# Weights of the first expert tile split by other engines, and two turns of rows moved by two steps

## Chip, core and metric

The kernel runs on one core of a Trainium2 chip. The metric is the device time of one execution in microseconds (us). Engines are named TensorE (PE, with its weight loads as PEld), VectorE (DVE), ScalarE (ACT), GpSimd (POOL) and SyncE (SP, which only issues transfers here).

## What is computed

Attention with rotary embedding over 4 batches, 8 heads, 576 tokens and 64 dimensions a head, and behind it a mixture of 8 experts with one expert for each token. A token keeps the expert of its predecessor unless its local gate is under 0.5.

```python
scores = scale * np.matmul(q_rot, k_rot.transpose(0, 1, 3, 2))
attn = softmax(scores)                    # over the keys
x = np.matmul(attn, v)                    # joined over the heads: 4 x 576 x 512
...
e = fresh_e if s == 0 or local_gate[b, s] < 0.5 else prev_e
h = np.maximum(x[b, s] @ w1[e], 0.0)      # 512 -> 1024
out[b, s] = p[e] * (h @ w2[e])            # 1024 -> 512
```

## The kernel before

The first part (to about 300 us) is the attention, 16 pairs of heads in 9 steps each. Its results go as rows to memory, and for the first three batches the tokens are sorted by expert. The second part works on tiles of 128 sorted tokens of one expert. The first six (`KE`) hold tokens of the first three batches alone, so that they can start while the routing of the fourth batch is still being worked out.

The work of a tile t:

- `gather(t)` (L893) fetches its 128 rows by an indirect DMA from POOL's queue.
- `turn_x(t)` transposes the rows on TensorE (L904, tile `tx`) and splits the result (L300 and L304): the high part of `xs` is a cast by ScalarE, the low part a subtraction by VectorE, with one input in PSUM and one in SBUF.
- `split_w(t, c)` makes high and low parts of pieces 2c and 2c+1 of the expert's eight weight pieces (128 x 1024 each; 0 to 3 are W1, 4 to 7 W2). The high part is a cast by ScalarE (L863) or an operation of POOL (L865), the low part a subtraction by VectorE or POOL (both L866), with both inputs in SBUF. `SPLITS[t]` says which: the first list names the pieces whose high part is ScalarE's, the second those whose low part is POOL's; all other high parts are POOL's, all other low parts VectorE's. For tile 0 the pieces 0 and 1 are split by POOL earlier (L835, L836). If a tile has the same expert as the one before, the split is skipped; only piece 0 and 1 of tile 1 are split whatever its expert.
- `first_product(t)` (L915, tile `h`) multiplies by W1, in four steps of six matmuls, one step for each piece: two with the high parts of rows and weights, two with the weights' low part, two with the rows' low part. A Relu (L919, tile `hr`) on ScalarE follows.
- `turn_h(t)` (L928, tiles `th`) transposes the inner rows, eight transposes, and splits them into `hs` as above.
- `second_product(t)` (L937, tile `o`) multiplies by W2, in four steps of six, and a scatter (L943) writes the rows.

The tiles overlap. For the first six, `TILE_EARLY[t]` is the order in which the steps are written down: f a step of the first product of tile t (the fifth is the Relu), s a step of the second product of tile t-1, x `turn_x(t + 1)`, A and B `split_w(t + 1, 0 and 1)`, C and D `split_w(t, 2 and 3)`, h `turn_h(t)`, g the gathers of tiles 4 and 5 at tile 0.

For these tiles TensorE and VectorE take their instructions in exactly this order; ScalarE, POOL and SP are ordered by a scheduler. In between stands the routing of the fourth batch (L467 to L611, small VectorE operations with a few TensorE and ScalarE ones). It has no place of its own in the string: each split by `split_to`, and each piece whose low part is VectorE's, first takes up to three of its operations (`pull(PULL)`). So a step that moves takes operations of the routing with it. The ones that matter here are, in this order, L467 and L485 (reductions), L488 (128 x 40, both inputs in SBUF), L491 (ScalarE), L496 and L498 (both inputs in SBUF), L501 (a reduction) and L504.

Of the kernel before, what the change touches and what calls it, by code (L numbers as in the profile page):

```python
# [44 lines left out]
QK_LAST = 121  # L45
SPREAD_LAST = 127

TILE_EARLY = ("ffAffsfxBssgCsshD", "ffAffxfsBsCsgsshD", "fffAffxBssChsgssD", "ffAfffxBsssshsCDg", "ffAfffBsssxsshCgD", "fffxAffsBssgssChD")
TILE = "ffAgffxBsfsshsCDs"
TILE_LAST = "ffxAfffssBsChsDss"  # L50
PULL = 3
# [5 lines left out]
DX = DM + 1  # L57
GATES_AT = {13: 4, 14: 7, 15: 4}

SPLITS = (((1, 2, 3, 4, 5, 7), (0, 6)), ((0, 3, 5, 6, 7), (1, 5, 6)), ((3, 4, 5, 6), (1, 5, 6)), ((1, 3, 4, 7), (1, 3, 4)), ((0, 2, 4, 5, 6), (5, 6)), ((3,), (0, 7)), ((2, 5, 6, 7), (4,)))  # L60
ACT_ROWS = False
ZTHR = -1.5 * 2.0 ** -23

# [72 lines left out]
def tile_attention_moe(ctx, tc, qk, v, tabs, turn, consts, tri, wg, wts, out):  # L136
# [162 lines left out]
    def split_to(hi, lo, src, wait=False):  # L299
        act.copy(hi, src)  # L300
        pull(PULL)

        def rest():
            dve.tensor_tensor(lo, src, hi.bitcast(F32), op=ALU.subtract)  # L304

        return rest if wait else rest()
# [100 lines left out]
    def finish():  # L407
        side["slots"] = 0
        for _ in side["parts"]:
            pass  # L410
# [397 lines left out]
    def expert_of(t):  # L808
        regs[t] = (
            sp.value_load(meta[0:1, t:t + 1], min_val=0, max_val=NE - 1),  # L810
            sp.value_load(meta[0:1, 32 + t:33 + t], min_val=0, max_val=1),
        )
# [29 lines left out]
    def needs_of(t):  # L842

        need_t[t] = nc.values_load_multi_w_load_instructions(
            meta[0:1, 32 + t:33 + t], engines=(act.engine, dve.engine, pool.engine), min_val=0, max_val=1)[1][0]

    def split_w(t, c):

        if c not in w_own:
            w = pt_p.tile([P, 2, 4, S], F32R, tag="pt", name=f"w_{c}")  # L850
            w_own[c] = w.rearrange("p a k s -> p (a k s)")[:, 0:4096].rearrange("p (c l n) -> p c l n", c=2, l=2)
            held = False
        else:
            held = t in need_t
        w = w_own[c]
        on_act, on_pool = SPLITS[min(t, KE)]

        def parts():
            for d in range(2):
                k = 2 * c + d  # L860
                src, hi, lo = staged(k), w[:, d, 0], w[:, d, 1]
                if k in on_act:
                    act.copy(hi, src)  # L863
                else:
                    pool.tensor_scalar(hi, src, 1.0, 1.0, op0=ALU.mult, op1=ALU.mult)  # L865
                (pool if k in on_pool else dve).tensor_tensor(lo, src, hi.bitcast(F32), op=ALU.subtract)  # L866

        for k in (2 * c, 2 * c + 1):
            if k not in on_pool:
                pull(PULL)  # L870
        if held:
            with tc.If(need_t[t] > 0):  # L872
                parts()
        else:
            parts()
        for d in range(2):
            k = 2 * c + d
            w_t[t, k] = w[:, d, 0], w[:, d, 1]
            w_done.add((t, k))
            load_w(t + 1, k)  # L880

    def gather(t):
        if t < 4:
            if t == 0:
                x_t[-1] = over.tile([P, 4, S], F32, tag="xq", name="x_0")
            x = x_t[-1][:, t]
        elif t < KE:
            x = over.tile([P, 1024], F32, tag=f"qst{t - 4}", name=f"x_{t}")
        else:
            x = xt_p.tile([P, S], F32, tag="xt", name=f"x_{t}")  # L890

        top = NT - S if t < KE else NT
        pool.indirect_dma_start(  # L893
            out=x[:, 0:DX], out_offset=None, in_=rows_d[0:top + 1],
            in_offset=bass.IndirectOffsetOnAxis(ap=gidx[:, t:t + 1], axis=0),
            bounds_check=top, oob_is_err=False)
        x_t[t] = x

    def turn_x(t, wait=False):
        xs = v2_p.tile([P, 10, 2, D], F32R, tag="v2", name=f"xs_{t}")  # L900
        xs = xs.rearrange("p j c d -> p (j c d)")[:, 0:1024].rearrange("p (l k n) -> p l k n", l=2, k=4)
        ps = ps_t.tile([P, 4, P], F32, tag="t", name=f"tx_{t}")
        for k in range(4):
            pe.transpose(ps[:, k], x_t[t][:, k * P:(k + 1) * P], ident)  # L904
        xs_t[t] = xs
        lo = split_to(xs[:, 0], xs[:, 1], ps, wait)
        return lo

    def first_product(t):
        ps = ps_s.tile([P, 2, 512], F32, tag="s", name=f"h_{t}")  # L910
        for k in range(4):
            w = w_t.pop((t, k))
            for n, (x, y) in enumerate(PASSES):
                for c in range(2):
                    pe.matmul(ps[:, c], xs_t[t][:, x, k], w[y][:, c * 512:(c + 1) * 512],  # L915
                              start=(k == 0 and n == 0), stop=(k == 3 and n == 2))
            yield k
        h = ej_p.tile([P, 2, S], F32, tag="ej", name=f"hr_{t}").rearrange("p a s -> p (a s)")[:, 0:1024]
        act.activation(h, ps.rearrange("p c n -> p (c n)"), AF.Relu)  # L919
        h_t[t] = h  # L920

    def turn_h(t):
        hs = m_p.tile([P, 2, 2, S], F32R, tag="m", name=f"hs_{t}")
        hs = hs.rearrange("p a c s -> p (a c s)")[:, 0:2048].rearrange("p (l k n) -> p l k n", l=2, k=8)
        for c in range(2):
            ps = ps_t.tile([P, 4, P], F32, tag="t", name=f"th_{t}_{c}")
            for k in range(4):
                pe.transpose(ps[:, k], h_t[t][:, (4 * c + k) * P:(4 * c + k + 1) * P], ident)  # L928
            split_to(hs[:, 0, 4 * c:4 * c + 4], hs[:, 1, 4 * c:4 * c + 4], ps)
        hs_t[t] = hs  # L930

    def second_product(t):
        ps = ps_t.tile([P, 512], F32, tag="t", name=f"o_{t}")
        for k in range(8):
            w = w_t[t, 4 + k // 2]
            for n, (x, y) in enumerate(PASSES):
                pe.matmul(ps, hs_t[t][:, x, k], w[y][:, (k % 2) * 512:(k % 2 + 1) * 512],  # L937
                          start=(k == 0 and n == 0), stop=(k == 7 and n == 2))
            if k % 2 == 1:
                yield k  # L940
        o = et_p.tile([P, S], F32, tag="et", name=f"os_{t}")
        act.activation(o[:, 0:DM], ps, AF.Copy, scale=x_t[t][:, DM:DM + 1])  # L942
        pool.indirect_dma_start(  # L943
            out=outf, out_offset=bass.IndirectOffsetOnAxis(ap=sidx[:, t:t + 1], axis=0),
            in_=o[:, 0:DM], in_offset=None, bounds_check=NT - 1, oob_is_err=False)
# [3 lines left out]
    def experts_phase():  # L949
        for t in range(LAST + 1):  # L950
            first = first_product(t)
            second = second_product(t - 1) if t > 0 else iter(())
            for c in TILE_LAST if t == LAST else TILE if t >= KE else TILE_EARLY[t]:
                if c == "f":
                    k = next(first, None)
                    if k == 1:
                        if t == KE - 1:
                            finish()
                        if t < LAST:
                            needs_of(t + 1)  # L960
                        if KE < t + 2 <= LAST:
                            expert_of(t + 2)
                    if k is not None:
                        yield t
                elif c == "s":
                    if next(second, None) is not None:
                        yield t
                elif c == "x" and t < LAST:
                    turn_x(t + 1)
                elif c in "AB" and t < LAST:  # L970
                    split_w(t + 1, "AB".index(c))
                elif c in "CD" and t > 0:
                    split_w(t, 2 + "CD".index(c))
                elif c == "h":
                    turn_h(t)
                    yield t + 1
                elif c == "g":
                    if t == 0:
                        gather(4)
                        gather(5)  # L980
                    elif KE < t + 2 <= LAST:
                        gather(t + 2)
        for _ in second_product(LAST):
            yield LAST
# [107 lines left out]
    if True:  # L1092
# [49 lines left out]
        for g in range(NSTEP):  # L1142
            with tc.manual_schedule(engines=None if g < GM else MAN0):
# [40 lines left out]
                if f:  # L1184
                    list(f())
        moe = experts_phase()
        with tc.manual_schedule(engines=MAN1):
            last = NPAIR - 1
# [102 lines left out]
```

## Time and profile before

| | |
|---|---|
| median of 3 runs | 557.57 us (556.94 to 559.15) |
| the profiled execution | 556.66 us, of which its span is 554.9 us |
| mean granted clock of TensorE in the span | 0.988 |
| busy in the span | TensorE 94%, VectorE 70%, ScalarE 61%, POOL 60% |
| tile 0's first product begins | 303.08 us |
| tile 1's first product begins | 310.83 us |

Times below are us from the start of the span. A row of the timeline gives start, length, engine, line, operation, tiles (out <- in) and count; rows of one kind that follow each other are merged, with their length from the first start to the last end. In brackets stands how long the engine was idle before the row, and what released it. A VectorE or POOL operation that is held by another shows as a longer operation, not as idle time. The granted clock is the share of TensorE's full clock.

### The profile page before, as it was taken

To read this page: it belongs to the slowest core of one execution; us is meant where nothing else is said; L and a number is where in the kernel's file an instruction comes from. 1 tells how busy PE (TensorE), PEld (TensorE's weight loads), DVE (VectorE), ACT (ScalarE), POOL (GpSimd) and SP (SyncE) were. 2 spreads that over 40 slices of the span, in tenths; PEclk is the share of its full clock that TensorE was granted. 3 is DMA by queue.
4 is the path that set the end of the run, shared out by engine and by line. 5 is a ranking of instruction groups with operands and counts; after the bars stand their busy time and mean duration, and the time that the engine had idled before them with its cause. 6 is when DMAs were issued, how large, how long until landed. Compare 5 with 4: busy or idle time off the path is not lost. (4 is left out here: it accounts for less than half of the span.)

```text
span 554.9 us, 10735 instructions
## 1 busy us (share of the span) xinstructions
PE 523.3 (94%) x3307; PEld 464.3 (84%) x3308; DVE 386.1 (70%) x714; ACT 337.9 (61%) x745; POOL 334.1 (60%) x245
## 2 busy tenths in 40 slices
PE   8779999999999999998999799999999999999991
PEld 4569989999999999997888578887888888888881
DVE  5978999999999999999999845346411535312540
ACT  3768989999999999987767324252522344423340
POOL 1996989878988988985698502355412444411331
PEclk9988999999999999999999999999999999999997
DMA  8838778877799787886397214553215464215130
GB/s 273 283 92 218 182 195 237 227 216 201 179 235 248 211 227 210 223 213 141 22 205 217 68 26 167 174 206 140 89 40 191 134 259 167 86 38 188 62 133 25
DMA packets 49831, 92.24 MB, mean 166 GB/s; under 512 B 15905, under 2 KB 26145, under 8 KB 47970
## 3 DMA queue, kind: packets, MB, share of 16 engines
q1 hardware_dynamic: 46722, 81.73, 52.5%
q0 software_dynamic: 3040, 9.71, 5.5%
q8 instruction: 29, 0.48, 0.4%
q14 instruction: 40, 0.33, 0.2%
HBM read 109.95 MB, written 9.71 MB: 216 GB/s over the span
## 5 line engine op out<-in xcount | busy, mean ns | idle before, releaser
L937 PE MATMUL o<-w,hs 128*128 128x512 f32 x456 | 113.1, 398 | 0.0
L269 DVE TENSOR_REDUCE mn<-s 128x1 f32<-128x576 f32 x144 | 107.2, 744 | 3.9 <-PE s L264 2.6
L915 PE MATMUL h<-w,xs 128*128 128x512 f32 x444 | 106.2, 393 | 2.7 <-DVE xs L304 2.4
L286 ACT ACTIVATE e<-s,mn 128x576 f32<-128x576 f32 x128 | 95.2, 744 | 19.4 <-DVE mn L269 17.0
L943 POOL DMA_INDIRECT out_dram<-os,sidx x19 | 23.1, 1215 | 129.2 <-ACT os L942 83.8
L264 PE MATMUL s<-m,qst 128*128 128x288 f32 x512 | 95.8, 309 | 4.8 <-ACT e L286 4.1
L915 PEld LDWEIGHTS h<-w,xs 128*128 128x128 f32 x444 | 82.5, 188 | 21.0 <-DVE xs L304 2.8
L304 DVE TENSOR_TENSOR ptl<-tm,pth 128x512 fp32r<-128x512 f32 x139 | 95.0, 684 | 6.7 <-ACT pth L300 3.0
L937 PEld LDWEIGHTS o<-w,hs 128*128 128x128 f32 x456 | 83.1, 188 | 17.0 <-DVE hs L304 0.4
L300 ACT CAST pth<-tm 128x512 fp32r<-128x512 f32 x139 | 80.8, 581 | 8.7 <-PE tm L322 7.3
L264 PEld LDWEIGHTS s<-m,qst 128*128 128x128 f32 x512 | 75.5, 191 | 9.1 <-ACT e L286 8.3
L322 PE MATMUL tm<-wid,e 128*128 128x128 f32 x512 | 77.9, 275 | 1.9 <-DVE ptl L304 0.9
L358 PE MATMUL pv<-pth,v 128*128 128x288 f32 x256 | 77.3, 317 | 1.2 <-DVE pkl L304 0.9
L358 PE MATMUL pv<-ptl,v 128*128 128x288 f32 x256 | 77.2, 317 | 0.0
L193 POOL TENSOR_TENSOR stage<-stage 128x1152 f32<-128x1152 f32 x26 | 69.3, 2669 | 6.5 <-DMA stage<-in_qk_dram 5.6
L866 DVE TENSOR_TENSOR w<-stage,w 128x1024 fp32r<-128x1024 f32 x40 | 55.0, 1413 | 25.4 <-POOL w L865 13.7
L322 PEld LDWEIGHTS tm<-wid,e 128*128 128x128 f32 x512 | 62.8, 141 | 3.1 <-DVE ptl L304 1.5
L304 DVE TENSOR_TENSOR hs<-th,hs 128x512 fp32r<-128x512 f32 x38 | 24.6, 684 | 42.6 <-ACT hs L300 40.1
L304 DVE TENSOR_TENSOR xs<-tx,xs 128x512 fp32r<-128x512 f32 x19 | 13.1, 689 | 57.9 <-ACTq L872 47.8
L358 PEld LDWEIGHTS pv<-pth,v 128*128 128x128 f32 x256 | 48.6, 190 | 4.8 <-DVE ptl L304 1.6
L358 PEld LDWEIGHTS pv<-ptl,v 128*128 128x128 f32 x256 | 48.8, 190 | 0.0
L300 ACT CAST xs<-tx 128x512 fp32r<-128x512 f32 x19 | 11.1, 586 | 61.8 <-PE tx L904 61.7
(188 smaller groups left out, 827.7 us busy)
## 6 DMA issues: line engine op xcount, KB each, us to landing
stage<-in_wts_dram SPq DMA_DIRECT2D x152, 512.0 KB
stage<-in_qk_dram SPq DMA_DIRECT2D x13, 1152.0 KB
qst<-xq SPq DMA_DIRECT2D x60, 128.0 KB
stage<-in_v_dram SPq DMA_DIRECT2D x16, 320.0 KB
m<-xk SPq DMA_DIRECT2D x16, 288.0 KB
m<-xk SPq DMA_DIRECT2D x16, 256.0 KB
m<-xq SPq DMA_DIRECT2D x14, 288.0 KB
m<-xq SPq DMA_DIRECT2D x14, 256.0 KB
```

The source lines that it names most:

```text
L193: engine.tensor_tensor(x, x, tab[:, 2 * f:2 * f + 2], op=ALU.mult)
L264: pe.matmul(st[:, h, lo:hi], lhs, keys[:, k0:k0 + hi - lo], start=(n == 0), stop=(n == len(parts_) - 1))
L269: dve.tensor_reduce(mn, s_t[g][:, :, 0:HALF], axis=AX.XY, op=ALU.min)
L286: act.activation(dst.rearrange("p (h s) -> p h s", h=2), s_t.pop(g)[:, :, 0:HALF], AF.Exp, bias=mn, scale=-1.0, accum_out=sums[:, col:col ...
L300: act.copy(hi, src)
L304: dve.tensor_tensor(lo, src, hi.bitcast(F32), op=ALU.subtract)
L322: pe.transpose(ps[:, k], src[:, k * P:(k + 1) * P], ident)
L358: pe.matmul(pv_t[p, u], lhs.rearrange("p c d -> p (c d)"), rhs, start=(n == 0), stop=(n == 9))
L866: (pool if k in on_pool else dve).tensor_tensor(lo, src, hi.bitcast(F32), op=ALU.subtract)
L915: pe.matmul(ps[:, c], xs_t[t][:, x, k], w[y][:, c * 512:(c + 1) * 512], start=(k == 0 and n == 0), stop=(k == 3 and n == 2))
L937: pe.matmul(ps, hs_t[t][:, x, k], w[y][:, (k % 2) * 512:(k % 2 + 1) * 512], start=(k == 0 and n == 0), stop=(k == 7 and n == 2))
L943: pool.indirect_dma_start(out=outf, out_offset=bass.IndirectOffsetOnAxis(ap=sidx[:, t:t + 1], axis=0), in_=o[:, 0:DM], in_offset=None, bou ...
```

## The change

```diff
-TILE_EARLY = ("ffAffsfxBssgCsshD", "ffAffxfsBsCsgsshD", ...
+TILE_EARLY = ("ffxAffsfBssgCssD", "ffiAffxfsBsCsgsshD", ...
...
-SPLITS = (((1, 2, 3, 4, 5, 7), (0, 6)), ...
+SPLITS = (((1, 2, 3, 4, 5, 6, 7), (0,)), ...
...
-                elif c == "h":
-                    turn_h(t)
+                elif c in "hi":
+                    turn_h(t - "hi".index(c))
                     yield t + 1
```

Piece 6 of tile 0's weights: its high part goes from POOL to ScalarE, its low part from POOL to VectorE. `turn_x(1)` stands behind the second step of tile 0's first product and ahead of `split_w(1, 0)`, where it stood behind the Relu. `turn_h(0)` stands behind the second step of tile 1's first product, where it stood ahead of the first.

TensorE, from the third step of tile 0's first product on (`h_5131` is tile 0's, `h_5231` or `h_5216` tile 1's; `tx` tile 1's rows, `th` tile 0's inner rows, `w_5156` or `w_5169` pieces 0 and 1 of tile 1). Before:

```order
L915 MATMUL h_5131<-w_5040,xs_5086 128x512 x12
L904 MATMUL tx_5183<-wid,x_4883 128x128 x4
L928 MATMUL th_0_5217<-wid,hr_5180 128x128 x4
L928 MATMUL th_1_5224<-wid,hr_5180 128x128 x4
L915 MATMUL h_5231<-w_5156,xs_5182 128x512 x5
L872 UNCONDITIONAL_BRANCH
L915 MATMUL h_5231<-w_5156,xs_5182 128x512
L520 MATMUL row_0_5238<-wid,key_5198 1x128 x4
L915 MATMUL h_5231<-w_5156,xs_5182 128x512 x6
L915 MATMUL h_5231<-w_5040,xs_5182 128x512 x12
```

The same place of the change:

```order
L904 MATMUL tx_5157<-wid,x_4883 128x128 x4
L915 MATMUL h_5131<-w_5040,xs_5086 128x512 x12
L915 MATMUL h_5216<-w_5169,xs_5156 128x512 x2
L872 UNCONDITIONAL_BRANCH
L915 MATMUL h_5216<-w_5169,xs_5156 128x512 x10
L520 MATMUL row_0_5241<-wid,key_5198 1x128 x4
L928 MATMUL th_0_5247<-wid,hr_5196 128x128 x4
L928 MATMUL th_1_5255<-wid,hr_5196 128x128 x4
L915 MATMUL h_5216<-w_5040,xs_5156 128x512 x6
L520 MATMUL row_1_5275<-wid,key_5198 1x128
L915 MATMUL h_5216<-w_5040,xs_5156 128x512 x6
```

Tile 1's rows are turned ahead of the 12 matmuls, and tile 0's inner rows behind the first 12 of tile 1.

VectorE, from the last weights of tile 0 on (`w_5114` and `w_5121` are pieces 4 to 7 of tile 0). Before:

```order
L866 TENSOR_TENSOR w_5114<-stage,w_5114 128x1024 x2
L866 TENSOR_TENSOR w_5121<-stage_4915,w_5121 128x1024
L844 TENSOR_LOAD meta
L467 TENSOR_REDUCE lg_all<-gm_4440 128x45
L485 TENSOR_REDUCE mx_5158<-lg_all 128x5
L488 TENSOR_TENSOR d_5160<-lg_all,mx_5158 128x40
L866 TENSOR_TENSOR w_5156<-stage,w_5156 128x1024
L496 SCALAR_TENSOR_TENSOR c_35_5191<-d_5160,cst 128x40
L498 SCALAR_TENSOR_TENSOR rs_5193<-lg_all,cst 128x5
L501 TENSOR_REDUCE f_5195<-c_35_5191 128x5
L304 TENSOR_TENSOR xs_5182<-tx_5183,xs_5182 128x512
```

The same place of the change:

```order
L866 TENSOR_TENSOR w_5114<-stage,w_5114 128x1024 x2
L866 TENSOR_TENSOR w_5121<-stage,w_5121 128x1024
L866 TENSOR_TENSOR w_5121<-stage_4915,w_5121 128x1024
L844 TENSOR_LOAD meta
L467 TENSOR_REDUCE lg_all<-gm_4440 128x45
L485 TENSOR_REDUCE mx_5164<-lg_all 128x5
L488 TENSOR_TENSOR d_5166<-lg_all,mx_5164 128x40
L304 TENSOR_TENSOR xs_5156<-tx_5157,xs_5156 128x512
L496 SCALAR_TENSOR_TENSOR c_35_5172<-d_5166,cst 128x40
L498 SCALAR_TENSOR_TENSOR rs_5174<-lg_all,cst 128x5
L501 TENSOR_REDUCE f_5176<-c_35_5172 128x5
L866 TENSOR_TENSOR w_5169<-stage,w_5169 128x1024
```

One L866 more stands at the front, and the low parts of `xs` and of tile 1's piece 0 have changed places around L496 to L501.

POOL, behind the gathers of tiles 0 to 3 (`x_5212` and `x_5208` are the rows of tiles 4 and 5). Before:

```order
L893 DMA x_4883<-rows_d,gidx 128x513 x4
L865 TENSOR_SCALAR w_5121<-stage 128x1024
L866 TENSOR_TENSOR w_5121<-stage,w_5121 128x1024
L893 DMA x_5212<-rows_d,gidx 128x513
L893 DMA x_5208<-rows_d,gidx 128x513
L865 TENSOR_SCALAR w_5156<-stage 128x1024
L866 TENSOR_TENSOR w_5156<-stage,w_5156 128x1024
```

The same place of the change:

```order
L893 DMA x_4883<-rows_d,gidx 128x513 x4
L893 DMA x_5212<-rows_d,gidx 128x513
L893 DMA x_5208<-rows_d,gidx 128x513
L865 TENSOR_SCALAR w_5169<-stage 128x1024
L866 TENSOR_TENSOR w_5169<-stage,w_5169 128x1024
```

The two operations on piece 6 are gone; the order of the rest stands. ScalarE's order has the cast of piece 6 ahead of that of piece 7, and the cast of `xs` of tile 1 ahead of that of tile 1's piece 0. SP's order is the same.

## Rows read from the trace of the kernel before

**Rows 1.** The page's first part: busy us, share of the span, instructions.

```profile
PE 523.3 (94%) x3307; PEld 464.3 (84%) x3308; DVE 386.1 (70%) x714; ACT 337.9 (61%) x745; POOL 334.1 (60%) x245
```

**Rows 2.** TensorE's waits, 302 to 320, then 320 to 555: total, times, longest.

```profile
PE h L915 <- DVE xs L304: 2.4, 1, 2.4
...
PE h L915 <- DVE w L866: 0.3, 1, 0.3
```

**Rows 3.** Timeline of TensorE, 306 to 315 us.

```profile
305.96 2.91 PE L915 MATMUL h<-w,xs 128*128 128x512 f32 x12
308.71 0.60 PE L904 MATMUL tx<-wid,x 128*128 128x128 f32 x4
309.99 1.09 PE L928 MATMUL th<-wid,hr 128*128 128x128 f32 x8 [0.68 <-ACT hr L919]
310.83 1.32 PE L915 MATMUL h<-w,xs 128*128 128x512 f32 x4
314.52 0.73 PE L915 MATMUL h<-w,xs 128*128 128x512 f32 x2 [2.37 <-DVE xs L304]
```

**Rows 4.** Timeline of VectorE, 305.6 to 314 us, and one later row.

```profile
305.60 1.22 DVE L866 TENSOR_TENSOR w<-stage,w 128x1024 fp32r<-128x1024 f32 x1
306.73 1.22 DVE L866 TENSOR_TENSOR w<-stage,w 128x1024 fp32r<-128x1024 f32 x1
307.87 0.82 DVE L467 TENSOR_REDUCE lg_all<-gm 128x45 f32<-128x360 f32 x1
...
308.96 1.27 DVE L488 TENSOR_TENSOR d<-lg_all,mx 128x40 f32<-128x40 f32 x1
310.15 1.21 DVE L866 TENSOR_TENSOR w<-stage,w 128x1024 fp32r<-128x1024 f32 x1
311.29 2.35 DVE L496 SCALAR_TENSOR_TENSOR c<-d,cst 128x40 f32<-128x40 f32 x1
313.56 0.15 DVE L498 SCALAR_TENSOR_TENSOR rs<-lg_all,cst 128x5 f32<-128x5 f32 x1
313.67 0.20 DVE L501 TENSOR_REDUCE f<-c 128x5 f32<-128x40 f32 x1
313.79 0.68 DVE L304 TENSOR_TENSOR xs<-tx,xs 128x512 fp32r<-128x512 f32 x1
...
380.83 1.21 DVE L866 TENSOR_TENSOR w<-stage,w 128x1024 fp32r<-128x1024 f32 x1
```

**Rows 5.** Timeline of POOL, 302 to 314 us, and one later gather.

```profile
302.18 2.39 POOL L866 TENSOR_TENSOR w<-stage,w 128x1024 fp32r<-128x1024 f32 x1
305.93 1.85 POOL L893 DMA_INDIRECT x<-rows_d,gidx  x1 [1.36 <-PE h L915]
308.09 1.00 POOL L893 DMA_INDIRECT x<-rows_d,gidx  x1 [0.30 <-issue]
309.12 1.06 POOL L865 TENSOR_SCALAR w<-stage 128x1024 fp32r<-128x1024 f32 x1
310.26 3.33 POOL L866 TENSOR_TENSOR w<-stage,w 128x1024 fp32r<-128x1024 f32 x1
...
381.36 1.59 POOL L893 DMA_INDIRECT x<-rows_d,gidx  x1 [0.64 <-POOLq L872]
```

**Rows 6.** Timeline of ScalarE: its casts of weights from 303 us on.

```profile
302.99 3.88 ACT L863 CAST w<-stage 128x1024 fp32r<-128x1024 f32 x4
```

**Rows 7.** Windows: stretch, its us, engines' busy us, granted clock, DMA share, GB/s.

```profile
29.00:30.00 1.00, 0.17 (x1) 0.20 (x2) 0.22 (x2) 0.73 (x5) 1.00 (x1) 0.70 0.83 193
30.00:31.00 1.00, 1.00 (x5) 1.00 (x6) 0.07 (x1) 0.00 (x0) 0.92 (x2) 0.50 0.86 197
...
32.00:33.00 1.00, 1.00 (x7) 1.00 (x6) 0.40 (x1) 0.56 (x1) 0.92 (x2) 0.60 0.72 259
...
315.00:316.00 1.00, 1.00 (x9) 0.75 (x7) 1.00 (x3) 0.00 (x0) 0.00 (x0) 1.00 0.00 0
```

**Rows 8.** Timeline of TensorE: its longest wait in the attention.

```profile
29.83 1.78 PE L264 MATMUL s<-xk,qtail 128*128 128x288 f32 x6 [3.36 <-ACT sum L426]
```

More of the change, by code (lines that the diff above doesn't have):

```diff
@@ L46 @@
 SPREAD_LAST = 127
-TILE_EARLY = ("ffAffsfxBssgCsshD", "ffAffxfsBsCsgsshD", "fffAffxBssChsgssD", "ffAfffxBsssshsCDg", "ffAfffBsssxsshCgD", "fffxAffsBssgssChD")
+TILE_EARLY = ("ffxAffsfBssgCssD", "ffiAffxfsBsCsgsshD", "fffAffxBssChsgssD", "ffAfffxBsssshsCDg", "ffAfffBsssxsshCgD", "fffxAffsBssgssChD")
 TILE = "ffAgffxBsfsshsCDs"
@@ L58 @@
 GATES_AT = {13: 4, 14: 7, 15: 4}
-SPLITS = (((1, 2, 3, 4, 5, 7), (0, 6)), ((0, 3, 5, 6, 7), (1, 5, 6)), ((3, 4, 5, 6), (1, 5, 6)), ((1, 3, 4, 7), (1, 3, 4)), ((0, 2, 4, 5, 6), (5, 6)), ((3,), (0, 7)), ((2, 5, 6, 7), (4,)))
+SPLITS = (((1, 2, 3, 4, 5, 6, 7), (0,)), ((0, 3, 5, 6, 7), (1, 5, 6)), ((3, 4, 5, 6), (1, 5, 6)), ((1, 3, 4, 7), (1, 3, 4)), ((0, 2, 4, 5, 6), (5, 6)), ((3,), (0, 7)), ((2, 5, 6, 7), (4,)))
 ACT_ROWS = False
```

## Prediction

> **What bounds the kernel now.** First the busy times: TensorE is busy for 523.3 of 554.9 us [rows 1], so only a stretch where it stands still, or is given work late, can move the time. Then the waits of TensorE in the part that the change touches and behind it. From 320 us to the end it waits 0.3 us in all; just before, there is one wait of 2.37 us, for the low part of the second tile's rows (`xs`), which VectorE makes [rows 2, 3]. So a delay or a gain at that place is carried unshortened to the end: nothing behind it has slack to swallow it.
>
> Then who is late there. TensorE's row order is in [rows 3]: first product of the first tile, rows of the second turned (L904), 0.7 us behind them the first tile's inner rows (L928, they need the Relu), four matmuls of the second tile, the wait, the rest. Beside it lie VectorE's rows [rows 4] and POOL's [rows 5]. They show a thing that decides the forecast: VectorE operations with both inputs in SBUF and POOL's splits exclude each other for their whole length. L488, 40 columns wide, takes 1.27 us and ends 0.05 us behind POOL's L865 (309.12 + 1.06 = 310.18). The L866 of VectorE then runs undisturbed in 1.21 us, and POOL's own L866 takes 3.33 us in place of the 2.39 of 302.18. L496, again 40 columns wide, takes 2.35 us and ends at 313.64, 0.05 us behind POOL's L866 (313.59). The low part of `xs` is queued behind L496; that is the wait of 2.37 us. L467 (a reduction) and L304 (one input in PSUM) are not held.
>
> **The change part by part.** *POOL loses two operations.* Piece 6 of the first tile's weights (L865 and L866, 1.06 and 2.39 us [rows 5]) goes: the high part to ScalarE, the low part to VectorE. POOL gains nothing from it, because behind that piece it waits for TensorE anyway: its next work, the gather at 305.93, starts when the matmuls on piece 1 are through, at 305.96 [rows 3, 5]. ScalarE's cast costs 0.97 us (3.88 / 4 [rows 6]); its row of casts then ends with piece 7 at about 306.9, and the casts that follow are wanted at 309.1, so this is hidden. If it were not, it would cost at most those 0.97 us. VectorE's extra L866 is not hidden: they stand 1.13 us apart (305.60, 306.73, and 307.87 for what follows [rows 4]), and the fourth pushes all behind it by 1.14 us. L467 now starts at 309.01, L488 at 310.10 (307.87 to 308.96 is 1.09).
>
> *The extra L866 also holds POOL.* The gather at 305.93 took 1.85 us and ended 0.96 us behind the L866 that ran when it came (305.60 + 1.22 = 306.82); the one at 381.36 ended 0.91 us behind its L866 (382.04); the one at 308.09 met none and took 1.00 [rows 4, 5]. With the change the second gather (308.09) meets the fourth L866 (307.87 to 309.09), so it ends at 309.09 + 0.94 = 310.03, and POOL's L865 for the second tile's piece 1 runs from 310.06 to 311.12, its L866 from 311.20 to 313.59.
>
> *The second tile's rows are turned earlier* (in front of 12 matmuls, not behind them). On VectorE their low part now stands ahead of L496 and ahead of the second tile's piece 0; L488 is held to 311.17, the low part is there at 311.78. That is 2.7 us earlier than before and removes the wait named above. What is late next is the thing that was moved behind: the low part of the second tile's piece 0. It stood ahead of L496 (310.15), now it stands behind it. L496 comes at 311.70, finds POOL in its L866 since 311.20, and ends at 313.64. L498 and L501 bring it to 313.79 (the same 0.15 us as before), then L866 runs to 315.00, and TensorE goes on 0.05 us later (314.47 to 314.52 before), at 315.05.
>
> *The first tile's inner rows are turned later*, two steps into the second tile. So TensorE has less to do before it must wait: from 305.96 it turns the second tile's rows (four transposes; the eight at 309.99 take 0.84 us, so 0.42), does 12 matmuls (2.75) and the two of the second tile that need high parts alone (0.46), and stands from about 309.6. The wait for ScalarE's Relu (0.7 us) is gone, but it would have been inside this wait. A wait of 5.4 us takes the place of 0.7 and 2.37.
>
> *The sum.* Before, at 314.52, TensorE had done the inner rows and four matmuls of the second tile. With the change, at 315.05, it lacks the inner rows (0.84) and two of the four matmuls (0.46). So it is 315.05 - 314.52 + 1.30 = 1.83 us behind. Everything that follows is ready in time: POOL's low part of piece 1 (313.59), the Relu (about 310.5), and the inner rows are wanted by the second product only 12 matmuls later.
>
> *The clock.* The trace has a wait of 3.36 us (before 29.83 [rows 8]); behind it the granted clock is 0.50 of full, that is 1.2 GHz and not 2.4, in the two slices from 30 to 32 us (one stands in [rows 7]), and in parts of the slices at 29 (mean 0.70) and 32 (0.60): 0.6 + 2 + 0.8 = 3.4 us in all, 3.0 of them with TensorE at work. Behind the wait of 2.37 us it was 1.00 [rows 7]. The new wait is longer than both, so I take the row at 29.83: 3.0 to 3.4 us of work at half speed, which cost 1.5 to 1.7 us; 1.6. The bounds are none (as at 314) and 2.4, if the clock stays low for a second such stretch.
>
> One page of the skill speaks against the step on the gather. The Trainium skill, SBUF — State Buffer, section "Who interferes with whom", says that a `tensor_tensor` takes only the read side of the port pair that VectorE shares with GpSimd, and infers that it does not hold up the building of DMA descriptors. The rows of the two gathers differ from this, and the measurement decides; what the sum would be by it is rival 2.
>
> **Forecast.** 556.66 us (the profiled execution: its span of 554.9 and 1.8 around it) + 1.83 + 1.6 = 560.1 us. Against the median of 557.57, which lies 0.9 above the profiled execution, that is 0.45% more. A measurement of this kernel tells some 0.5% (2.8 us) from no change, so the verdict would be "no change", with the bound at 560.4 close above.
>
> **Rivals.** *1. The clock holds.* For it: the 2.37 us that left it at 1.00. Against it: the 3.36 us, and that the new wait is longer by 2 us. 556.66 + 1.83 = 558.5.
>
> *2. The gather is not held by an L866.* Then POOL's L865 starts at 309.12 as before, its L866 runs from 310.26 to 312.65, L496 ends at 312.70, piece 0 at 314.06, and TensorE goes on at 314.11: 0.89 us behind. With the clock's fall 559.2, without it 557.6. Against it: two rows out of two. By the page named above this would be the result.
>
> *3. Slower: the clock stays low for longer.* The wait of 5.4 us is longer than a whole low stretch of 3.4 us, so the fall can come early in the wait and a second stretch can follow it, with TensorE at half speed from 315.05 for up to some 4.9 us: 2.4 us lost, 560.9. It decides once over 3.8 us of work are done at half clock, since 556.66 + 1.83 + 1.9 passes 560.4. Against it: the low stretch behind 29.83, which also began in a wait, came singly [rows 7, 8].
>
> *4. VectorE comes first.* If POOL's L865 came 1.2 us later still, L488, `xs`, L496, L498 and L501 would go through unheld and the L866 for piece 0 be done near 312.4. But then POOL's L866 for piece 1 would start behind it, end at 314.8, and TensorE, there at 312.47 + 6 x 0.23 = 313.85, would wait 0.95 us. Net 312.47 + 1.30 + 0.95 - 314.52 = +0.2, 556.9. The change then does what its order says, at no gain. A real gain (under 554.8) needs both held operations to vanish, and no row speaks for that.
>
> **How the numbers follow.** Forecast 0.55, rival 1 0.12, rival 2 0.08, rival 3 0.15, rival 4 0.08, a gain from what no row shows 0.02. The predicted time is the forecast's, 560.1. Its own range is 559.3 to 560.9: the runs shown differ by 2.2 us among themselves, and some of that will lie on either side. The range for all is 557.4 to 561.5; it leaves out rival 4, the gain and the end of rival 3, and takes in 1 and 2. Slower by over 0.5%: rival 3 and about two fifths of the forecast, 0.37. Faster by over 0.5%: 0.02. The rest, 0.61, within.
>
> **What would show it right or wrong.** Right: the wait of TensorE for `xs` is gone, and one of some 5.4 us stands between the second and third matmul of the second tile, released by VectorE's L866; L496 lasts about 2 us and ends with POOL's L866; the gather that starts near 308.1 lasts 1.9 and not 1.0 us; the granted clock is 0.50 in a stretch that ends some microseconds behind 315; behind that the matmuls stand as before, shifted. Wrong: a wait under 3 us there (rival 4, or VectorE before POOL), a gather of 1.0 us (rival 2), a clock of 1.00 throughout (rival 1). The whole reading is wrong if TensorE shows a new wait behind 320 us, or if the second product waits for the inner rows that are now turned later.

## The result, and the profile after

The changed kernel takes 560.69 us (median of 6 runs, 559.88 to 561.9); the kernel before, run beside it, 557.86 us (6 runs). The ratio is 1.0053, with a 95% interval of 1.003 to 1.0076. So it is slower by about half a per cent, clear of no change. The profiled execution took 561.9 us, its span 560.1, against 556.66 and 554.9 before.

The busy times hardly moved [rows 1]. Page of the changed kernel, part 1:

```profile
PE 523.5 (93%) x3307; PEld 464.0 (83%) x3308; DVE 386.5 (69%) x715; ACT 339.1 (61%) x746; POOL 329.9 (59%) x243
```

POOL has lost two operations, ScalarE and VectorE have gained one each, and TensorE does the same work. The time is in where TensorE stands still, and in its clock. Its waits from 302 to 320 us, and from 330 us to the end (what is waited for, total, times, longest):

```profile
PE h L915 <- DVE w L866: 5.2, 1, 5.2
...
PE h L915 <- DVE w L866: 0.3, 1, 0.3
```

The wait of 2.37 us for `xs` and the 0.68 us for the Relu [rows 2, 3] are gone; one wait of 5.2 us for a low part of the weights has come. Behind 330 us there is the same 0.3 us as before, so whatever is lost at this place is carried to the end. Timeline of TensorE at the place:

```profile
307.25 0.60 PE L904 MATMUL tx<-wid,x 128*128 128x128 f32 x4
307.60 3.45 PE L915 MATMUL h<-w,xs 128*128 128x512 f32 x14
316.23 4.63 PE L915 MATMUL h<-w,xs 128*128 128x512 f32 x10 [5.17 <-DVE w L866]
...
321.51 1.08 PE L928 MATMUL th<-wid,hr 128*128 128x128 f32 x8
...
325.67 3.00 PE L937 MATMUL o<-w,hs 128*128 128x512 f32 x12
```

The rows of tile 1 are turned, then come the last 12 matmuls of tile 0 and the first two of tile 1 in one row (x14), then the wait, and only behind it the inner rows of tile 0 (L928). The ten matmuls behind the wait take 4.63 us, 0.46 each; the 12 at 305.96 before took 2.91, 0.24 each [rows 3]. That is half speed, and the windows show why (columns as in [rows 7]):

```profile
314.00:315.00 1.00, 0.00 (x0) 0.00 (x0) 1.00 (x4) 0.00 (x0) 0.76 (x1) 0.89 0.30 74
315.00:316.00 1.00, 0.00 (x0) 0.00 (x0) 1.00 (x2) 0.00 (x0) 0.00 (x0) 0.50 0.01 4
...
321.00:322.00 1.00, 1.00 (x9) 0.83 (x7) 0.25 (x1) 0.00 (x0) 0.00 (x0) 0.70 0.00 0
```

The granted clock falls in the slice from 314 us, in which TensorE does nothing, and is back after 321.6 (0.70 in the slice from 321 is three fifths at half speed): 6.8 us at 0.50, of which 316.23 to 321.6, 5.4 us, have TensorE at work. Work at half speed loses half of its time, so 2.7 us by this estimate.

To compare kernels, the text takes the stretch from the first matmul or transpose behind the 12 matmuls on pieces 0 and 1 of tile 0 (305.96 before, 307.25 after) to the start of tile 0's second product, its first `o` row. Before, that row of TensorE's timeline is:

```profile
320.10 3.02 PE L937 MATMUL o<-w,hs 128*128 128x512 f32 x12
```

The stretch is 320.10 - 305.96 = 14.14 us before and 325.67 - 307.25 = 18.42 after: 4.28 us longer. The two spans differ by 5.2 us: 1.29 because the stretch starts later, 4.28 in the stretch, and some -0.4 behind it. The 1.29 come from the attention, where every engine's operations stand in the same order in both traces. Near its beginning, at 53 us, TensorE has a wait for a transfer that before doesn't have,

```profile
PE s L264 <- DMA qst<-xq: 2.0, 1, 2.0
```

Such a wait doesn't go with the change: below, the split alone has one of 1.3 us, and the first experiment under "POOL's part" has none. Over the ten profiled executions of this document the start of the stretch lies between 305.26 and 308.15, for kernels with the changed order between 305.58 and 308.15; the text takes this as a spread between executions, though one profile of each kernel can't show that. Below, "the stretch" is always this one, and its 14.14 us are what each kernel is compared with.

Who holds whom is in VectorE's and POOL's rows. VectorE:

```profile
305.75 4.62 DVE L866 TENSOR_TENSOR w<-stage,w 128x1024 fp32r<-128x1024 f32 x4
...
311.38 1.00 DVE L488 TENSOR_TENSOR d<-lg_all,mx 128x40 f32<-128x40 f32 x1
312.31 0.68 DVE L304 TENSOR_TENSOR xs<-tx,xs 128x512 fp32r<-128x512 f32 x1
312.91 1.90 DVE L496 SCALAR_TENSOR_TENSOR c<-d,cst 128x40 f32<-128x40 f32 x1
...
314.96 1.22 DVE L866 TENSOR_TENSOR w<-stage,w 128x1024 fp32r<-128x1024 f32 x1
```

POOL:

```profile
307.70 1.27 POOL L893 DMA_INDIRECT x<-rows_d,gidx  x1 [6.03 <-PE h L915]
309.27 1.97 POOL L893 DMA_INDIRECT x<-rows_d,gidx  x1 [0.31 <-PE h L915]
311.27 1.06 POOL L865 TENSOR_SCALAR w<-stage 128x1024 fp32r<-128x1024 f32 x1
312.42 2.34 POOL L866 TENSOR_TENSOR w<-stage,w 128x1024 fp32r<-128x1024 f32 x1
```

Four L866 instead of three stand on VectorE, to 310.37. The second gather comes at 309.27, meets the fourth, and lasts 1.97 us where it lasted 1.00 [rows 5]. POOL's two splits for tile 1's piece 1 follow it. L488 is held to 312.38, 0.05 us behind the L865 (311.27 + 1.06 = 312.33). L496 ends at 314.81, 0.05 behind POOL's L866 (314.76). Behind L496 stands the L866 for tile 1's piece 0, for which TensorE waits. Had the stretch begun at 305.96 as before, TensorE would have gone on at 316.23 - 1.29 = 314.94, 0.42 us later than before, with 1.30 us of work (inner rows and two matmuls) still to do that was done by then before. So the order of the work costs about 1.7 us (314.94 - 314.52 + 1.30), and the clock the rest of the 4.28, about 2.5.

### The profile page after: what moved, and what is told of

Same layout as the page of the kernel before. It is cut to its first block, busy times and chain, and to the rows that moved or that the text cites. A ratio compares the mean times of both kernels' runs of the same rounds, so it can differ in the third digit from the quotient of the medians.

```text
span 560.1 us, 10733 instructions
## 1 busy us (share of the span) xinstructions
PE 523.5 (93%) x3307; PEld 464.0 (83%) x3308; DVE 386.5 (69%) x715; ACT 339.1 (61%) x746; POOL 329.9 (59%) x243
## 5 line engine op out<-in xcount | busy, mean ns | idle before, releaser
L915 PE MATMUL h<-w,xs 128*128 128x512 f32 x444 | 108.1, 398 | 5.5 <-DVE w L866 5.5
L915 PEld LDWEIGHTS h<-w,xs 128*128 128x128 f32 x444 | 83.8, 191 | 24.2 <-DVE w L866 6.7
L866 DVE TENSOR_TENSOR w<-stage,w 128x1024 fp32r<-128x1024 f32 x41 | 56.0, 1405 | 25.4 <-POOL w L865 13.7
```

## The experiments

All compare with runs of the kernel before on the same chip. There were two chips, on which it took 557.39 and 556.85 us, so kernels are compared by their ratios to it; a ratio is worked out from all runs and need not be that of the two medians. Each profile is of one execution. Each figure "on before's times" is a time of the profile less the difference between the two starts of the stretch.

### Each half of the change alone

*The split alone.* Against the kernel before:

```diff
-SPLITS = (((1, 2, 3, 4, 5, 7), (0, 6)), ...
+SPLITS = (((1, 2, 3, 4, 5, 6, 7), (0,)), ...
```

> Piece 6 alone goes from POOL to ScalarE and VectorE, the order is that of before. Theory A (VectorE and POOL exclude each other): the fourth L866 pushes L467 by 1.1 us and holds the second gather to about 1.9 us; L488 ends with POOL's L865, tile 1's piece 0 comes next, POOL's L866 behind it, L496 is held to the end of that, the low part of xs is done some 1.0 us later than before, and TensorE's wait for it grows from 2.4 to about 3.4 us: 557.7 us with the clock held, about 559 if it falls. Theory B (the extra work of VectorE and ScalarE is what costs, POOL does not matter): the gather takes 1.0 us, L496 keeps its 2.35 us, the wait grows by 1.1 us. Theory C (only the order costs): 556.7 us as before.

Measured: 559.18 us (7 runs) against 557.39, ratio 1.0035 (1.0021 to 1.005). TensorE's timeline:

```profile
305.26 2.91 PE L915 MATMUL h<-w,xs 128*128 128x512 f32 x12
...
311.59 0.73 PE L915 MATMUL h<-w,xs 128*128 128x512 f32 x2 [0.75 <-DVE w L866]
314.69 1.22 PE L915 MATMUL h<-w,xs 128*128 128x512 f32 x2 [2.36 <-DVE xs L304]
...
323.06 3.02 PE L937 MATMUL o<-w,hs 128*128 128x512 f32 x12
```

POOL's:

```profile
307.29 1.97 POOL L893 DMA_INDIRECT x<-rows_d,gidx  x1 [0.30 <-issue]
```

The order is that of before, and the wait for `xs` did not grow to 3.4 us as expected: it stayed at 2.36, and a new wait of 0.75 us for piece 0 stands ahead of it. TensorE goes on 314.69 - 305.26 = 9.43 us into the stretch where it was 314.52 - 305.96 = 8.56: 0.87 us later, where 1.0 was expected. The fourth L866 on VectorE holds the second gather, and the gather all of POOL behind it. The stretch is 17.80 us, 3.66 longer, because the clock was low from 313.84 to 320.66 as well. Behind the wait of 2.36 us here the clock was low, behind the one of 2.37 us before it was not.

*The order alone.* Against the changed kernel:

```diff
-SPLITS = (((1, 2, 3, 4, 5, 6, 7), (0,)), ...
+SPLITS = (((1, 2, 3, 4, 5, 7), (0, 6)), ...
```

> The two turns are moved, piece 6 stays with POOL. Theory A: the second gather is free of an L866 and takes 1.0 us, POOL's L865 starts about 0.9 us earlier than in the changed kernel, L496 is still held to the end of POOL's L866, tile 1's piece 0 is ready about 314.1, TensorE waits some 4.5 us and is 0.9 us behind before: 557.6 us with the clock held, 559 to 560 with its fall. Theory C (the order is the whole cost): as the changed kernel, 560 to 561 us. If moving the turns helped, under 556.

Measured: 559.18 us (12 runs) against 557.39, ratio 1.003 (1.0015 to 1.0045). TensorE's timeline:

```profile
307.39 0.60 PE L904 MATMUL tx<-wid,x 128*128 128x128 f32 x4
...
315.51 4.63 PE L915 MATMUL h<-w,xs 128*128 128x512 f32 x10 [4.31 <-DVE w L866]
...
325.31 3.00 PE L937 MATMUL o<-w,hs 128*128 128x512 f32 x12
```

POOL's:

```profile
309.52 1.00 POOL L893 DMA_INDIRECT x<-rows_d,gidx  x1 [0.30 <-PE h L915]
```

With three L866 on VectorE the second gather is 1.00 us long. TensorE goes on at 314.08 on before's times, 0.44 earlier than before, but lacks 1.30 us of work: 0.86 behind. The stretch is 17.92, 3.78 longer, again with a low stretch of the clock (314.78 to 321.61). So neither half alone is the culprit: each puts TensorE some 0.9 us behind (the two together 1.7 to 1.8), and each sends it into a wait behind which the clock is low.

### The clock by itself

*Keep TensorE busy in the wait.* Twenty matmuls whose output nobody reads are put into the wait of the changed kernel; all else is the same.

```diff
+                if t == 1 and k == 0 and n == 0:
+                    idle = ps_t.tile([P, 512], F32, tag="t", name="idle_ps")
+                    for _ in range(20):
+                        pe.matmul(idle, onesb, ohr[:, 0:4]..., start=True, stop=True)
```

> The changed kernel, with 20 matmuls of 512 bfloat16 columns into a bank that nobody reads, between the second and third matmul of tile 1: TensorE is at work in most of its wait, and they end before piece 0 comes. Theory A: the granted clock stays 1.00 through the place, TensorE goes on at the same time, and the kernel is 1.7 to 2.7 us faster than the changed one: about 558.4 us, some 1.8 us over the profiled execution of before. If the low clock is a mark of the wait and costs nothing by itself: 560.7 as the changed kernel.

Measured: 557.9 us (12 runs) against 557.39, ratio 1.0013 (0.9997 to 1.003). TensorE's timeline:

```profile
307.82 0.60 PE L904 MATMUL tx<-wid,x 128*128 128x128 f32 x4
...
311.47 4.49 PE L920 MATMUL idle_ps<-ohr,onesb 128*128 128x512 bf16 x19
316.81 2.56 PE L915 MATMUL h<-w,xs 128*128 128x512 f32 x10 [0.85 <-DVE w L866]
...
323.77 3.00 PE L941 MATMUL o<-w,hs 128*128 128x512 f32 x12
```

Its windows:

```profile
317.00:318.00 1.00, 1.00 (x5) 0.82 (x5) 0.00 (x0) 0.00 (x0) 0.00 (x0) 1.00 0.00 0
```

The ten matmuls behind the wait now take 2.56 us, not 4.63, at a clock of 1.00, and the stretch is 15.95 us: 1.81 longer than before. This is the order's cost with the clock taken out, and the prediction had 1.83. The rest of the changed kernel's 4.28 us, 2.47, is the clock's. Between the two ratios, 1.0013 here and 1.0053 for the changed kernel, lie 0.40%, some 2.2 us; by their intervals it can be 0.7 to 3.8. The mean granted clock of all executions says the same: 0.9875 here, 0.984 in the changed kernel.

*The same in the kernel before.* Nine such matmuls in its wait of 2.37 us (with `n == 1`).

> The kernel before, with 9 matmuls of 512 bfloat16 columns into a bank that nobody reads, in its wait of 2.4 us for xs; they end before the wait does. The changed kernel with its wait filled stood only 0.7 us over the median of before, though its profile puts it 1.8 us later at the place. Theory D: before loses its clock at this wait in some of its executions (not in the profiled one), so with the wait filled it is about 1 us faster: ratio near 0.998. If it never does: ratio 1.000, and the 1.1 us that are missing have another cause.

Measured: 555.94 us (12 runs) against 556.85 (35 runs), ratio 0.9989 (0.9976 to 1.0001). TensorE's timeline:

```profile
311.38 2.12 PE L920 MATMUL idle_ps<-ohr,onesb 128*128 128x512 bf16 x9
313.92 0.73 PE L915 MATMUL h<-w,xs 128*128 128x512 f32 x2 [0.42 <-DVE xs L304]
```

The stretch is 14.15 us (305.35 to 319.50), 0.01 off, as it should be where the clock held anyway [rows 7]. The median is 0.9 us lower and the ratio 0.11%, at the edge of what can be told. The single executions say more. Of the 35 of the kernel before, 15 have a mean granted clock of 0.980 to 0.985 and a median of 557.65 us; the other 20 have 0.986 to 0.992 and a median of 556.54. With the wait filled, all 12 have 0.986 to 0.990. So the kernel before probably loses clock at this place in some four of ten executions, at about 1.1 us each, and its profiled one is one in which it didn't. That would be part of why the medians of the two kernels (2.8 us apart) differ less than their profiled stretches (4.28). No profile of the kernel before shows such an execution, so the place stays a reading of times and mean clocks.

### POOL's part

*Take the split of tile 1's piece 1 from POOL.* Its high part goes to ScalarE and its low part to VectorE, in the changed kernel:

```diff
-SPLITS = (..., ((0, 3, 5, 6, 7), (1, 5, 6)), ...
+SPLITS = (..., ((0, 1, 3, 5, 6, 7), (5, 6)), ...
```

> The changed kernel, but the second tile's piece 1 goes from POOL to ScalarE and VectorE, so that POOL does nothing but gathers here; the routing's operations stand where they stood (one more, L504, and its transposes come ahead of piece 0). Theory A (it is POOL's L866 that holds L496): L488 and L496 take 0.2 us each, piece 0 is ready about 312.8 on the times of before, and TensorE is 0.8 us ahead of before there: 555.9 us with the clock held, about 558 if it falls, since it still waits some 3 us. Theory B (VectorE's amount of work is what counts, and here it has one L866 more still): 561 us or over.

Measured: 556.67 us (12 runs) against 556.85, ratio 0.9993 (0.9978 to 1.0009). VectorE's timeline:

```profile
309.69 0.20 DVE L488 TENSOR_TENSOR d<-lg_all,mx 128x40 f32<-128x40 f32 x1
...
310.40 0.19 DVE L496 SCALAR_TENSOR_TENSOR c<-d,cst 128x40 f32<-128x40 f32 x1
...
310.94 2.36 DVE L866 TENSOR_TENSOR w<-stage,w 128x1024 fp32r<-128x1024 f32 x2
```

L488 and L496 take 0.20 and 0.19 us in place of 1.00 and 1.90: the 2.5 us were POOL's. The stretch is 15.32 us (305.58 to 320.90), 1.18 longer, though with a low clock for 3.4 us (some 1.7 of loss) and five small matmuls (L534, 0.39) that came into it from behind; less these it is by this estimate 0.9 shorter than before, where 0.8 was expected. TensorE's wait here was 2.24 us, for the routing's `key` (L504); the clock fell 1.3 us behind its end.

*Leave POOL's split, and move the routing instead.* The routing's operations are not taken up between `turn_x(1)` and `split_w(1, 0)`, so that L467 to L501 come behind tile 1's piece 0:

```diff
-            if side["slots"] > 0:
+            if side["slots"] > 0 or side.get("hold"):
...
+                side["hold"] = t == 0 and c in "xA"
```

> The changed kernel with POOL's piece 1 left in place, but the turn and the split in tile 0's string take no routing operations: the low parts of xs and piece 0 stand ahead of L467. Theory A: piece 0 is ready about 310.8, but POOL's L865 and L866 for piece 1 come behind VectorE's L866 and end about 314.3, so the wait moves to piece 1: some 1.2 us for piece 0, then 2 us for piece 1, and TensorE 0.2 us ahead of before: 556.4 us with the clock held, 558 to 559 if it falls. If POOL did not matter: 3.5 us ahead of before, 553 us.

Measured: 557.17 us (12 runs) against 556.85, ratio 1.0004 (0.9984 to 1.0024). VectorE's timeline:

```profile
311.80 2.52 DVE L866 TENSOR_TENSOR w<-stage,w 128x1024 fp32r<-128x1024 f32 x1
```

POOL's:

```profile
310.18 1.97 POOL L893 DMA_INDIRECT x<-rows_d,gidx  x1 [0.30 <-PE h L915]
312.18 1.06 POOL L865 TENSOR_SCALAR w<-stage 128x1024 fp32r<-128x1024 f32 x1
313.32 3.23 POOL L866 TENSOR_TENSOR w<-stage,w 128x1024 fp32r<-128x1024 f32 x1
```

TensorE's:

```profile
314.37 4.29 PE L915 MATMUL h<-w,xs 128*128 128x512 f32 x10 [2.42 <-DVE w L866]
```

The time is in the range expected, but the place was missed. TensorE should have gone on at 310.8 on before's times and did at 312.2. The L866 for piece 0 comes at 311.80, while the second gather is still running (to 312.15); when that ends, POOL's L865, which follows within 0.03 us, gets in first (to 313.24), and the L866 ends 1.08 us behind that, at 314.32; it had its turn only then, and POOL's own L866 waits for it in its turn (3.23 us). So it is not the small operations that matter: an L866 in their place is held as they were. The stretch is 14.80 (308.15 to 322.95), 0.66 longer, with 3.4 us at the low clock.

*Both, without the split of piece 6.* `SPLITS[0]` is that of the kernel before, `SPLITS[1]` that of the experiment before last, the strings are the changed ones, and the routing is held back as above.

> The turns moved as in the change, piece 6 with POOL as before; tile 1's piece 1 goes from POOL to ScalarE and VectorE, and the turn and the split of piece 0 and 1 in tile 0's string take no operations of the routing, which come behind them. Theory A (what costs is that piece 0 stands behind L496 and that POOL's L866 holds L496): VectorE makes xs, piece 0 and piece 1 without being held, piece 0 is ready near 309.7, TensorE waits under 0.5 us, the clock stays: 3.5 us under before, about 553 us. If the moved turns cost by themselves (inner rows late for the second product): a wait in front of the second product, and not under 556 us.

Measured: 554.16 us (6 runs) against 557.39, ratio 0.9937 (0.9922 to 0.9952): faster than both kernels. TensorE's timeline:

```profile
307.72 0.60 PE L904 MATMUL tx<-wid,x 128*128 128x128 f32 x4
308.07 6.03 PE L915 MATMUL h<-w,xs 128*128 128x512 f32 x24
...
318.37 3.00 PE L937 MATMUL o<-w,hs 128*128 128x512 f32 x12
...
325.02 0.47 PE L534 MATMUL ec<-wid,sc 1*128 1x1 f32 x5 [0.78 <-ACTq L872]
```

ScalarE's:

```profile
324.28 0.69 ACT L942 ACTIVATE os<-o,x 128x512 f32<-128x512 f32 x1 [4.57 <-PE o L937]
```

VectorE's:

```profile
309.62 0.69 DVE L304 TENSOR_TENSOR xs<-tx,xs 128x512 fp32r<-128x512 f32 x1
310.23 2.35 DVE L866 TENSOR_TENSOR w<-stage,w 128x1024 fp32r<-128x1024 f32 x2
```

Twenty-four matmuls stand in a row without a wait. Right behind the low part of `xs` VectorE makes both low parts of tile 1's first pieces, in 1.18 us each, since POOL has no split there. The stretch is 10.65 us, 3.49 shorter than before (3.5 was expected): its two waits (0.68 and 2.37) are gone. Of that 0.78 us come back in a new wait, ahead of matmuls of the routing (L534) that now come behind tile 0's second product and not in its middle; it ends when ScalarE has scaled that product's output (L942, to 324.97). So the moved order can stand in a kernel that gains. No run moves POOL and the routing in the old order, so how much of the 0.6% the moved turns bring is not shown.

### The second turn

*The inner rows back at their old place.* `turn_h(0)` stands ahead of tile 1's first product again; the rest of the change stays.

```diff
-TILE_EARLY = ("ffxAffsfBssgCssD", "ffiAffxfsBsCsgsshD", ...
+TILE_EARLY = ("ffxAffsfBssgCsshD", "ffAffxfsBsCsgsshD", ...
```

> The changed kernel with the first tile's inner rows turned where they were in before (behind the Relu, ahead of tile 1's first matmul). Theory A: piece 0 comes at the same 315.05 on the times of before, but the eight transposes (0.84 us) lie inside the wait and not behind it: 0.84 us faster than the changed kernel, some 559.8 us, TensorE 1.0 us behind before at the place. If the clock then holds more often, since the wait is split by the transposes, down to 558. If moving the inner rows helped in itself: over 561.

Measured: 558.57 us (12 runs) against 556.85, ratio 1.0045 (1.0025 to 1.0065). TensorE's timeline:

```profile
311.35 1.10 PE L928 MATMUL th<-wid,hr 128*128 128x128 f32 x8 [1.11 <-ACT hr L919]
...
315.87 1.20 PE L915 MATMUL h<-w,xs 128*128 128x512 f32 x4 [2.96 <-DVE w L866]
...
321.92 2.99 PE L937 MATMUL o<-w,hs 128*128 128x512 f32 x12
```

Its windows:

```profile
316.00:317.00 1.00, 1.00 (x5) 0.72 (x6) 0.96 (x2) 0.00 (x0) 0.00 (x0) 1.00 0.00 0
```

With the inner rows inside it, the long wait falls into two (1.11 and 2.96 us), and 1.6 us of work lie between (the eight transposes and two matmuls, 311.35 to 312.91). In this execution the clock held, and the stretch is 15.05: 0.91 longer, 1.0 expected. So by the profiles moving the inner rows behind the wait cost 1.81 - 0.91 = 0.9 us of the order's 1.8, about their own length (0.84). The times don't confirm it: the ratio is 0.08% under the changed kernel's where 0.15% was expected, and the two intervals overlap. The profiled execution had a mean clock of 0.991, the 12 timed ones 0.984 on average, and the three slowest (561.3 to 562.45 us) 0.977 to 0.980. So in most executions this kernel probably loses clock too; no profile shows where.

## Why the prediction came out as it did

The forecast was 560.1 us, 0.45% more than before; measured were 560.69 us and 0.53%, inside the range. That the two lie so close is in part luck, as two mistakes cancelled (below). "Within 0.5%" was given the larger chance, 0.61; the ratio lies a little past that bound, with its interval on both sides of it.

| step of the prediction | predicted | measured |
|---|---|---|
| POOL gains nothing from losing piece 6 | gather starts when piece 1's matmuls are through | it waited 6.03 us for them |
| second gather held by the fourth L866 | 1.94 us | 1.97 |
| L496 held by POOL's L866 | 1.94 us | 1.90 |
| wait for `xs` gone, one for piece 0 in its place | 5.4 us | 5.17 |
| TensorE goes on, on before's times | 315.05 | 314.94 |
| cost of the order | 1.83 us | 1.81 (clock kept up) |
| cost of the clock | 1.6 us | 2.5 in the profile, 2.2 (0.7 to 3.8) by the ratios |

**Right: the chain of holds and the order's cost.** Each link came within 0.25 us of the row that it was read from, and the experiments take the links apart: without POOL's split the holds vanish (0.20 and 0.19 us), without the fourth L866 the gather is 1.00 us and TensorE 0.86 us behind, where the same chain had given 0.89 (rival 2), and with the inner rows put back 0.9 us return in the profile.

**Mis-sized: the clock.** The step that failed is the choice of one low stretch of 3.4 us, from the wait of 3.36 us in the attention [rows 7, 8]. In the profiled execution the low stretch was 6.8 us, and 5.4 of them met work: that is rival 3, which was given 0.15. Its price had been put at 2.4 us, close to what came; that the fall would come early in the wait was not so, it came some 3.7 us into it and 1.4 us before its end. The trace of before also had a second low stretch, which the prediction left out:

```profile
42.73 0.37 PE L358 MATMUL pv<-pth,v 128*128 128x288 f32 x1 [0.74 <-DVE pkl L304]
```

```profile
43.00:44.00 1.00, 1.00 (x6) 1.00 (x5) 1.00 (x3) 0.66 (x3) 1.00 (x1) 0.52 0.88 184
```

The clock stood at 0.50 from 43.0 to 46.5 us, 3.4 us again, behind waits of 0.93 and 0.74 us, while behind the 2.37 it stayed up. So already the trace of before shows that the length of a wait alone doesn't tell whether the clock falls, and the prediction had gone by that length.

**What the prediction took for granted: that the kernel before loses none.** It read from one execution that the clock holds behind the wait of 2.37 us. The experiments have waits of 2.36 us (with 0.68 and 0.75 us ahead of it) and of 2.42 us behind which the clock was low, and one of 2.96 us behind which it held, so one execution with the clock up is no proof that it stays up. The runs of the kernel before with its wait filled speak for some 0.5 to 0.9 us lost there on the average: clearly by the mean clocks, by the times only at the edge of their interval. This mistake made the forecast of the difference too large, the one on the low stretch made it too small, and the two nearly cancelled on the medians. That is luck.

**Rivals 1 and 2 fell.** Rival 1 (the clock holds, 558.5) needed a clock of 1.00, which behind this wait only the busy wait gave. Rival 2 needed a gather of 1.0 us; it took 1.97 with a fourth L866 beside it and 1.00 without. This is against what the Trainium skill, SBUF — State Buffer, section "Who interferes with whom", infers for a `tensor_tensor` and the building of descriptors; the traces here have the gather held, in the changed kernel, with the split alone and with the routing behind (1.97 us each). The gathers are indirect, and POOL also takes their row numbers (`gidx`) from SBUF; no run here separates that from the building of descriptors, so what in the gather is held stays open. Rival 4 (VectorE ahead of POOL, no gain) was not what happened. In the experiment that let piece 0 go ahead of the routing VectorE still came second, because POOL's L865 followed the gather at once.

**What stays open.** Which waits lose the clock, and why some low stretches last 3.4 us (two experiments, and both of before's) and others 6.8 (three kernels), can't be read from these runs: wait lengths alone don't sort them.

## What to carry to other kernels

Ahead of a move of work between engines, list which operations exclude each other for their whole length, and follow that queue as one engine: here VectorE's two-input operations and POOL's splits and gathers were one queue, and a 40-column operation of 0.2 us took 1.9 because of its place in it. Price a wait of TensorE in two parts, what the order costs and what the clock costs behind it, and separate them with throw-away matmuls in the wait; as the clock can differ between executions of one kernel, look at the mean clock of many and not only at the one profiled. Ahead of moving a step forward, look at what then stands in front of the next step: the same turns, with piece 6 back at POOL, tile 1's piece 1 off POOL and the routing behind, went from 0.5% slower to 0.6% faster.

## What was not expected of the hardware

- Matmuls that nobody reads made the kernel faster: with 20 of them in a wait of 5.17 us the granted clock stayed at 1.00 behind it, and the ratio fell by 0.40%. The expectation of that run had it, the prediction had no word of it.
- The hold between POOL and VectorE goes on at the end of a gather: an L866 of VectorE that came during one had its turn not when it ended but behind POOL's following L865, and took 2.52 us in place of 1.2 (one execution).
- Waits of nearly the same length (2.36, 2.37 and 2.42 us) had the clock low, up, and low behind them, and waits of under 1 us had it low (43.0 to 46.5 us of before).
